# Strided attention heads with block-diagonal keys and values, in a fused sparse-attention and bilinear-FFN kernel

## The chip, the cores and the metric

The kernel runs on one core of a Trainium2 chip. The metric is the device time of one execution in microseconds; before the change the median of three runs is 328.93 (328.39 to 329.02). A core has TensorE (PE, matmuls, with its weight loads listed as PEld), VectorE (DVE), ScalarE (ACT), GpSimd (POOL), SyncE (SP) and 16 DMA engines. POOL and SP issue the transfers here.

## What is computed

Sparse attention over 8 batches, 8 heads, 576 positions and 64 values a head, and then a bilinear feed-forward layer. Heads 0 to 3 are local (a query sees the 32 latest positions), heads 4 to 7 strided (a query sees the earlier positions with the same remainder by 32).

```python
    mask_local = (rel >= 0) & (rel < stride)
    mask_strided = (rel >= 0) & (pos[None, :] % stride == pos[:, None] % stride)
    masks = np.stack([mask_local if h < H // 2 else mask_strided for h in range(H)], axis=0)
    scores = np.where(masks[None, :, :, :], scores, -1000000000.0)
...
    a = x @ w_a
    b = x @ w_b
    return (a * b @ w_out).astype(np.float32)
```

`x` is the attention's output, 4608 tokens of 512 values; `w_a` and `w_b` are 512 x 1536, `w_out` 1536 x 512.

## The kernel before, in words

**The order of the work.** Everything is one list of 144 slots, nine token tiles of 512 tokens with 16 slots each: 12 slots of `ffn_ab` (L584; per slot eight matmuls of 512 columns, L581, an ACT copy L598 and a DVE product L601 or L603) and four of the output product (`ffn_y` L762 for the first two tiles, `ffn_ys` L750 for the rest, a Strassen-like scheme whose sums DVE forms in `fast_s` L608, matmuls L686). Attention of batch b is woven into the slots of earlier tiles by hand: `STEPS` (L541) for batches 1 and 2, `LATER` (L546) for 3 to 7 give a position for each step; batch b's `LATER` positions count from slot 16(b-1), x.5 lies in the middle of slot x+1. `at` (filled from L884 on) gives, for each slot, the loads, transpositions and small jobs emitted behind it. Each engine runs its instructions in the order in which they are emitted. From slot 14 on, POOL first copies one element of the slot's result (`pace`, L936) before it issues what `at` has for the slot, so that loads don't run ahead.

**A batch from 2 on.** A batch has 8 units: unit u is pair c = u // 2 of heads, half u % 2; pairs 0 and 1 are local, 2 and 3 strided. A step "S" forms scores (`S_p`, L385) into the one score bank `st`, takes Exp (L393) into one of five buffers `p` and masks by a bitwise AND (L403). A step "V" (`step_VT`, L475) multiplies by the values (L486) into the one output bank `o`; half of the 128 weight columns are ones, so that partitions 64 to 127 of `o` hold the sums. ACT turns these into 1/sum by Ln and Exp (L495, L496), and DVE multiplies into `xT` (L500 for local, L502 for strided units), the FFN's input.

**Strided units before.** The 576 positions of a head are cut as 72 rows of 8 (`NP`, `RS`): in group r lie the positions that leave r by 8, 72 keys and 72 queries, and the mask `mask_s` keeps those with the same remainder by 32. A unit has 4 groups of 2 heads: eight score matmuls (weights: 128 columns of the transposed keys `kT`, moving: 72 queries of `qz`, zero outside of one head) and eight value matmuls (weights `vs`, 72 x 128; moving: 72 columns of `p`). Keys and queries are loaded by POOL (`load_qk`, L203, tiles `natk`, `natq`, once for all four heads, one DMA each head), transposed by DVE in 32 x 32 blocks, three instructions for each (`step_D`, L332), and sent by SP's DMAs (L342, L346) into `kT` and `qz`. Values are loaded by `load_vs` (L243), one DMA a head. Local heads go the same way: `kl`, `ql` (L212), transposed in two instructions (L327).

Batches 0 and 1 use other code for transposition and values, and are not changed; they share the buffers. `rezero` (L349), `zero_qz` (L113) and `fill_v` (L108) put zeros and ones into the buffers at their start or before the first use by a batch from 2 on. `mask_group` (L138) builds `mask_s` by a matmul.

Of the kernel before, what the change touches and what calls it, by code (L numbers as in the profile page):

```python
# [7 lines left out]
F32 = mybir.dt.float32  # L8
# [17 lines left out]
WCH = (0, 2, 5, 9, 12)  # L26
FAST_Y = (2, 3, 4, 5, 6, 7, 8)
# [3 lines left out]
def kernel(  # L31
# [44 lines left out]
    def qk_buf(nm):  # L76
        return (const.tile([128, 2, S], BF16, name=f"{nm}l"), const.tile([128, 2, RS * GP], BF16, name=f"{nm}s"))

    qz_buf = [[qk_buf(f"qz{i}{j}") for j in range(2)] for i in range(2)]
# [4 lines left out]
    nat_s = {nm: const.tile([128, 3, RS * D], BF16, name=f"nat{nm}") for nm in "qk"}  # L84
    p_buf = [const.tile([128, 2, PW], BF16, name=f"p{i}") for i in range(5)]
    vs_buf = [const.tile([NP, HL, RS, VW], BF16, name=f"vs{i}") for i in range(2)]
# [11 lines left out]
    def consts(i):  # L98
        if i == 0:
            for p in p_buf:  # L100
                nc.vector.memset(p[:, :, W:], 0.0)
        nc.vector.memset(kT_buf[i][0][:, :, 0:PAD], 0.0)
        nc.vector.memset(kT_buf[i][1], 0.0)
        nc.vector.memset(vl_buf[i][:, :, D:D + 1], 1.0)
        nc.vector.memset(vs_buf[i][:, :, :, D:D + 1], 1.0)
        nc.vector.memset(vl_buf[i][:PAD, 0, 0:D], 0.0)

    def fill_v(t):  # L108
        nc.gpsimd.memset(t[:, :, :, D:] if len(t.shape) == 4 else t[:, :, D:], 1.0)
# [28 lines left out]
    def mask_group(part):  # L138

        if part == 0:  # L140
            nc.scalar.copy(by4(nm_l[lo, :NP]), ident[lo, :NP // 4].unsqueeze(2).to_broadcast([32, NP // 4, 4]))
            nc.scalar.copy(by4(nm_l[up, :NP]), ident[up, 32:36].unsqueeze(1).to_broadcast([32, NP // 4, 4]))
            nc.scalar.copy(nm_l[64:], nm_l[:64])
        elif part == 1:
            nc.vector.tensor_scalar(nm_r[up], nm_l[up, :NP], 1.0, 8e9, op0=ALU.subtract, op1=ALU.mult)
            nc.vector.tensor_copy(nm_r[64:], nm_r[:64])
        else:
            mp = cur["misc"][:NP, 256:256 + NP]
            nc.tensor.matmul(mp, lhsT=nm_l[:, :NP], rhs=nm_r, start=True, stop=True)
            nc.vector.tensor_scalar(mask_s, mp, 0.0, -1.0, op0=ALU.is_equal, op1=ALU.mult)  # L150

# [35 lines left out]
    def load_qk(b, strided, heads=range(HL), names="kq"):  # L187
        for nm in names:
            src = {"k": k, "q": q}[nm]
            if b < FIRST_D:  # L190
                n, R, h0 = (NP, RS, HL) if strided else (96, RL, 0)
                w0 = {"k6": 0, "q6": 1536, "k8": 3072, "q8": 5120}[f"{nm}{R}"]
                if b not in shared:
                    shared[b] = nat.tile([128, FG * 5 * SW], BF16, tag="shared", name="shared")
                t = nats[b, nm, strided] = shared[b][:n, w0:w0 + HL * R * D].rearrange("p (h r d) -> p h r d", r=R, d=D)
                hs = slice(heads[0], heads[-1] + 1)
                nc.gpsimd.dma_start(out=t[:, hs], in_=src[b, h0:h0 + HL].rearrange("h (p r) d -> p h r d", r=R)[:, hs])  # L197
            elif strided:

                t = nat_s[nm]  # L200
                n = 32 if b == FIRST_D else YS
                for h in heads:
                    nc.gpsimd.dma_start(  # L203
                        out=t[32 * h:32 * h + n],
                        in_=bass.AP(tensor=src.tensor, offset=(b * H + HL + h) * S * D,
                                    ap=[[RS * D, n], [YS * RS * D, 3], [1, RS * D]]))
            else:
                if 0 in heads:
                    nats[b, nm, strided] = nat.tile([128, NY, D], BF16, tag=f"{nm}l", name=f"{nm}l")
                t = nats[b, nm, strided]  # L210
                for h in heads:
                    nc.gpsimd.dma_start(out=t[32 * h:32 * h + 32],  # L212
                                        in_=src[b, h].rearrange("(i y) d -> y i d", y=32))
            nats[b, nm, strided] = t
# [18 lines left out]
    def load_vs(b, heads=range(HL)):  # L233
        if b < FIRST_D:

            for z in range(2):
                t = blocks("k", z)
                nc.gpsimd.dma_start(out=t[:NP, :, :RS * D],
                                    in_=v[b, HL + 2 * z:HL + 2 * z + 2].rearrange("h (p r) d -> p h (r d)", r=RS))
                nats[b, "v", z] = t  # L240
            return
        for h in heads:
            nc.gpsimd.dma_start(out=vs_buf[b % 2][:, h, :, 0:D],  # L243
                                in_=v[b, HL + h].rearrange("(p r) d -> p r d", r=RS))
# [74 lines left out]

    def step_D(b, z, nm, part):  # L320
        src = nats[b, nm, z == 1]
        if part == 0:
            tl[b, z, nm] = blocks(nm, z)
        t = tl[b, z, nm]
        if z == 0:
            i = slice(NY // 2 * part, NY // 2 * (part + 1))
            nc.vector.transpose(t.rearrange("p h (i y) -> p i h y", i=NY)[:, i],  # L327
                                src[:, i].rearrange("p i (h d) -> p i h d", h=2))
            last = part == 1
        else:  # L330

            nc.vector.transpose(  # L332
                t.rearrange("p h (r c) -> p r h c", r=RS)[:, :, :, YS * part:YS * part + 32],
                src[:, part].rearrange("p (r h d) -> p r h d", r=RS, h=2))
            last = part == 2
        if last:
            for nm, c in {"k": (("k", 0),), "q": (("q", 0), ("k", 1), ("q", 1))}[nm]:
                t = tl[b, z, nm]
                for e in range(2):
                    if nm == "k":  # L340
                        dst = kT_buf[b % 2][z][64 * e:64 * e + 64, c]
                        nc.sync.dma_start(out=dst[:, PAD:] if z == 0 else dst[:, :RS * GP], in_=t[64 * c:64 * c + 64, e])  # L342
                        continue
                    for j in range(2):
                        r0 = 64 * c + 32 * j
                        nc.sync.dma_start(out=qz_buf[b % 2][j][z][64 * e + 32 * j:64 * e + 32 * j + 32, c],  # L346
                                          in_=t[r0:r0 + 32, e])

    def rezero(b):  # L349

        for j in range(2):
            for t in qz_buf[b % 2][j]:
                nc.gpsimd.memset(t[32:64] if j == 0 else t[64:96], 0.0)
# [35 lines left out]
    def S_x(b, u):  # L389
        c, half, M, n, G = unit(u)  # L390
        st = held.pop((b, "st", u))
        p = ps[b, u] = p_buf[(B * b + u) % 5]
# [15 lines left out]

    def step_S(b, u):
        S_px(b, u)  # L410
        S_m(b, u)
# [55 lines left out]
    def step_V(b, u):  # L467
        if b >= FIRST_D:
            step_VT(b, u)
# [5 lines left out]
    def step_VT(b, u):  # L475
# [4 lines left out]
        for i in range(G):  # L480
            for j in range(2):
                if c < 2:
                    vt = vl_buf[b % 2][:, (2 * c + j) * 6 + 3 * half + i]
                else:
                    vt = vs_buf[b % 2][:, 2 * (c - 2) + j, 4 * half + i]
# [4 lines left out]
        if c < 2:  # L490
            sums = o[64:, :, :W]
        else:

            sums, r = (t.rearrange(e, p=NP) for t, e in ((o[64:, :, :W], "d j (g p) -> d j p g"), (r, "d j (p g) -> d j p g")))
        nc.scalar.activation(r, sums, ACT.Ln)  # L495
        nc.scalar.activation(r, r, ACT.Exp, scale=-1.0)  # L496
        for j in range(2):
            dst = xT[64 * j:64 * j + 64, c, S * (b % XR):S * (b % XR + 1)]
            if c < 2:
                nc.vector.tensor_mul(dst[:, W * half:W * (half + 1)], o[:64, j, :W], r[:, j])  # L500
            else:
                nc.vector.tensor_mul(dst.rearrange("d (p r) -> d p r", r=RS)[:, :, G * half:G * (half + 1)],  # L502
                                     o[:64, j, :W].rearrange("d (g p) -> d p g", p=NP), r[:, j])
# [21 lines left out]
    def step_X(b, c):  # L525
# [18 lines left out]
             2: {20: "S0", 20.5: "S1", 21.5: "V0", 22: "S2", 23: "V1", 23.5: "S3", 24.5: "V2", 25: "S4", 26: "V3", 26.5: "S5",  # L544
                 27.5: "V4", 28: "S6", 28.5: "V5", 29: "S7", 29.5: "V6", 30.5: "V7"}}
    LATER = {-1: "S0", 0: "S1", 1: "V0", 2: "S2", 3: "V1", 4: "S3", 5: "V2", 6: "S4", 7: "V3", 8: "S5", 9: "V4", 10: "S6",  # L546
             11: "V5", 12: "S7", 12.5: "V6", 14: "V7"}
# [249 lines left out]
    with tc.manual_schedule(engines={ENG.PE, ENG.SP, ENG.Pool, ENG.DVE, ENG.Activation}):  # L797
# [87 lines left out]
        do(0, fill_v, vs_buf[0])  # L885
# [3 lines left out]
        for b in range(FIRST_D, B):  # L889
# [7 lines left out]
            else:  # L897
                for h in range(HL):
                    do(g0 + h + (2 if b == FIRST_D + 1 else -2), load_qk, b, False, (h,))
# [3 lines left out]
            gs = {2: (14, 14, 15, 15, 16, 16, 17, 17, 18, 18), 3: (8, 9, 10, 11, 12, 13, 14, 15, 16, 17)}.get(b) or (  # L903
                3, 5, 7, 9, 12, 13, 14, 15, 16, 17)
            for (z, nm, part), g in zip(((0, "k", 0), (0, "k", 1), (0, "q", 0), (0, "q", 1), (1, "k", 0), (1, "k", 1),
                                         (1, "k", 2), (1, "q", 0), (1, "q", 1), (1, "q", 2)), gs):
# [10 lines left out]
        do(28, fill_v, vs_buf[1])  # L917
# [52 lines left out]
```

## Time and profile before

| what | value |
|---|---|
| median of three runs | 328.93 us |
| span of the profiled execution | 326.3 us |
| PE busy, instructions | 320.6 us (98%), 2820 |
| DVE busy | 265.7 us (81%) |
| ACT busy | 202.7 us (62%) |
| POOL busy | 177.2 us (54%) |
| PE busy between 20 and 262 us | 242.00 of 242 us |
| POOL waiting at `pace` for DVE's `pf` (L601) | 80.7 us, 53 times |

The span runs from the first to the last instruction; the time of an execution also holds its start and end. The profile gives busy time by engine, the span in 40 slices, the chain of waits that ended last, and groups of instructions by line with their mean duration. A PE duration is that of one matmul from start to result; matmuls overlap, so the spacing of their starts tells what each costs. A line that is used by several shapes or tiles has a group for each in the list by form.

### The profile page before, as it was taken

The page shows a single profiled execution, that of the slowest core. Times are in us where ns is not written, and L with a number is a line of the kernel's source. Part 1 is how long each engine was busy: PE and PEld are TensorE (multiplying, and loading weights), DVE is VectorE, ACT ScalarE, POOL GpSimd, SP SyncE. Part 2 cuts the span into 40 slices and gives each one's busy share as a digit, 9 for nine tenths or more (in the row PEclk, how much of TensorE's full clock was granted, in tenths as well). Part 3 has the DMA queues.
Part 4 walks back from the last instruction along what each step waited for, and adds up shares of the span by engine and source line. Part 5 has one row for each costly group of instructions (what it writes and reads, how often), then busy time and mean ns, then how long its engine had stood idle before and what let it go on. Part 6 is the DMA issues. An engine that isn't in the chain of part 4 may idle for free.

```text
span 326.3 us, 7676 instructions
## 1 busy us (share of the span) xinstructions
PE 320.6 (98%) x2820; PEld 205.5 (63%) x2820; DVE 265.7 (81%) x509; ACT 202.7 (62%) x329; POOL 177.2 (54%) x295
## 2 busy tenths in 40 slices
PE   8999999999999999999999999999999999999995
PEld 6754655455555587557999985569555954584474
DVE  6766888889778999999999999999877845647562
ACT  6764775478778765777677757875677643313321
POOL 8935839599966655875577557853312031232021
PEclk9999999999999999999999999999999999999999
DMA  9999999999999798799979999898033022004004
GB/s 151 154 204 201 204 184 182 173 171 136 132 213 116 95 97 79 77 217 125 83 72 199 138 86 77 160 180 84 20 77 115 2 67 64 0 2 129 1 2 129
DMA packets 98869, 37.50 MB, mean 115 GB/s; under 512 B 76688, under 2 KB 96016, under 8 KB 98832
## 3 DMA queue, kind: packets, MB, share of 16 engines
q0 software_dynamic: 85968, 19.48, 64.5%
q1 hardware_dynamic: 12576, 17.34, 18.4%
q8 instruction: 22, 0.36, 0.4%
q10 hardware_dynamic: 288, 0.20, 0.2%
q14 instruction: 15, 0.12, 0.1%
HBM read 39.51 MB, written 9.44 MB: 150 GB/s over the span
## 4 chain that ended last, share of the span: by engine, by line
PE 96%; DMA 2%; POOL 0%; DVE 0%; issue 0%; POOLq 0%; ACT 0%; DVEq 0%
PE mm L581 56%; PE mm L686 17%; PE mm L768 6%; PE st L385 5%; PE o L486 4%; DMA shared<-in_q_dram 2%; PE mm L714 2%; PE o L442 1%; PE ab L581 1%; PE misc L154 1%; PE tp L511 1%; PE tp L296 1%; PE end L714 1%; PE tp L287 0%; POOL shared L197 0%
## 5 line engine op out<-in xcount | busy, mean ns | idle before, releaser
L581 PE MATMUL mm<-xT,wa_sb 128*128 128x512 bf16 (+1 forms) x472 | 110.3, 357 | 0.0
L581 PE MATMUL mm<-xT,wb_sb 128*128 128x512 bf16 (+1 forms) x472 | 110.3, 357 | 0.0
L598 ACT COPY a_sb<-mm 128x512 f32<-128x512 f32 x106 | 62.1, 586 | 48.3 <-PE mm L581 47.6
L936 POOL CAST pace<-pf 1x1 f32<-1x1 bf16 x84 | 31.4, 374 | 84.0 <-DVE pf L601 80.7
L581 PEld LDWEIGHTS <-wb_sb 128*128 128x128 bf16 x480 | 46.3, 98 | 44.0 <-issue 0.2
L601 DVE TENSOR_TENSOR pf<-a_sb,mm 128x512 bf16<-128x512 f32 x84 | 56.4, 672 | 17.0 <-PE mm L581 13.8
L581 PEld LDWEIGHTS <-wa_sb 128*128 128x128 bf16 x480 | 42.7, 98 | 31.3
L393 ACT ACTIVATE p<-st 128x576 bf16<-128x576 f32 (+1 forms) x64 | 41.6, 650 | 11.7 <-PE st L385 11.1
L495 ACT ACTIVATE xr<-o 64x576 f32<-64x576 f32 x48 | 31.1, 649 | 25.0 <-PE o L486 24.2
L686 PEld LDWEIGHTS <-ps 128*128 128x128 bf16 x360 | 34.6, 98 | 3.9
L496 ACT ACTIVATE xr<-xr 64x576 f32<-64x576 f32 x48 | 32.9, 685 | 1.5
L500 DVE TENSOR_TENSOR xT<-o,xr 64x288 bf16<-64x288 f32 x48 | 21.5, 447 | 7.2 <-ACT xr L496 6.7
L502 DVE TENSOR_TENSOR xT<-o,xr 64x288 bf16<-64x288 f32 x48 | 21.5, 448 | 6.2 <-ACT xr L496 5.1
L686 PE MATMUL mm<-wf,ps 128*128 128x256 bf16 x216 | 26.4, 273 | 0.0
L768 PE MATMUL mm<-wo_sb,pf 128*128 128x512 bf16 x96 | 23.4, 379 | 0.0
L403 DVE TENSOR_TENSOR p<-p,mask_l 128x576 int16<-128x576 int16 x32 | 22.2, 694 | 1.2 <-ACT p L393 1.1
L243 POOL DMA_DIRECT2D vs<-in_v_dram x24 | 19.7, 821 | 3.0 <-PE st L385 2.2
L212 POOL DMA_DIRECT2D kl<-in_k_dram x24 | 16.1, 671 | 5.5 <-issue 3.6
L212 POOL DMA_DIRECT2D ql<-in_q_dram x24 | 16.0, 666 | 5.2 <-DMA wo_sb<-in_moe_w_out_dram 3.8
L603 DVE TENSOR_TENSOR pf<-a_sb,mm 128x512 bf16<-128x512 f32 x22 | 14.9, 676 | 4.3 <-ACT a_sb L598 2.8
L936 POOL COPY pace<-y_sb 1x1 f32<-1x1 f32 x16 | 2.8, 177 | 27.8 <-ACT y_sb L669 15.1
L686 PE MATMUL mm<-wf,pf 128*128 128x256 bf16 x144 | 17.6, 273 | 0.0
(162 smaller groups left out, 502.1 us busy)
## 6 DMA issues: line engine op xcount, KB each, us to landing
out_dram<-y_sb SPq DMA_DIRECT2D x12, 512.0 KB, 4.6
out_dram<-y_sb SPq DMA_DIRECT2D x10, 256.0 KB, 3.3
vl<-in_v_dram POOLq DMA_DIRECT2D x6, 384.0 KB, 6.8
kl<-in_k_dram POOLq DMA_DIRECT2D x24, 72.0 KB, 3.0
ql<-in_q_dram POOLq DMA_DIRECT2D x24, 72.0 KB, 3.0
vs<-in_v_dram POOLq DMA_DIRECT2D x24, 72.0 KB, 3.7
wo_sb<-in_moe_w_out_dram POOLq DMA_DIRECT2D x4, 384.0 KB, 9.2
natk<-in_k_dram POOLq DMA_DIRECT2D x20, 72.0 KB, 3.3
```

The source lines that it names most:

```text
L212: nc.gpsimd.dma_start(out=t[32 * h:32 * h + 32], in_=src[b, h].rearrange("(i y) d -> y i d", y=32))
L393: nc.scalar.activation(p[:M, :, :W], st[:M, :, :W], ACT.Exp, scale=scale)
L403: nc.vector.tensor_tensor(pi, pi, mk, op=ALU.bitwise_and)
L495: nc.scalar.activation(r, sums, ACT.Ln)
L496: nc.scalar.activation(r, r, ACT.Exp, scale=-1.0)
L500: nc.vector.tensor_mul(dst[:, W * half:W * (half + 1)], o[:64, j, :W], r[:, j])
L581: nc.tensor.matmul(ps_[:, c0:c0 + n], lhsT=w[:, kk, 128 * f:128 * (f + 1)], rhs=xT[:, kk, x0:x0 + n], start=(kk == first and c0 == 0), sto ...
L598: nc.scalar.copy(a_sb, ab[0])
L601: nc.vector.tensor_mul(pf[:, f, :].rearrange("p (i a s) -> p a i s", i=2, s=16), halves(a_sb), halves(ab[1]))
L686: nc.tensor.matmul(bank[b][:, q], lhsT=lhs(g, q), rhs=rhs(g), start=new and q == 0 and g == 0, stop=g == FG - 1, skip_group_check=True)
L768: nc.tensor.matmul(ybank[j], lhsT=pf[:, f, 128 * j:128 * (j + 1)], rhs=wo_sb[:, f], start=(f == 0), stop=(f == FD - 1))
L936: nc.gpsimd.tensor_copy(pace, done)
```

## The change

For batches 2 to 7 the strided heads are cut otherwise. Positions are placed at 33 i + x (i = 0 to 17 the row of 32, x = 0 to 31 the remainder, x = 32 a zero pad), read as 54 keys n times 11 groups g: in a group lie the 54 positions with x in {g, g + 11, g + 22}. For a pair of heads one matmul takes 2 x 54 = 108 keys, both heads' keys block-diagonal in the weights (`kz`), against 54 queries of both heads: 11 score matmuls a pair (`pair_S`), their output 108 x 594. Both operands are read with a step of 11 elements. Exp is taken in two instructions (324 and 270 columns), the mask is one of 108 x 54 (`mask_z`). `pair_V` multiplies by block-diagonal values (`vz`, 108 x 128, head 0 in columns 0 to 63, head 1 in 64 to 127), 6 or 5 matmuls of 54 columns, and a constant block of ones (`ones_z`) gives the sums in one matmul of 324 or 270 columns. Ln and Exp then run on 128 partitions of 324 or 270, and two multiplications write both heads.

Steps S5 and S7 go (S4 and S6 do a pair each), V4 moves from position 9 to 8.5, S6 from 10 to 9, V5 from 11 to 10 (batch 2: V4 stays at 27.5, S6 at 28, V5 at 28.5). Strided keys and queries are loaded as the local ones are (576 pieces of a row a head, where it was 72, or 96 in batch 2), and transposed in two instructions instead of three, after a small memset of the pad; queries now go to `kT`, keys to `kz`. The value load of a head becomes three DMAs. The local loads of batch 3 move one slot earlier. New at the start: `zero_vz` in place of `fill_v` of `vs`, and `mask_pair` in three parts (slots 0, 15, 18: POOL memsets and selects; four ACT copies and a DVE operation; one matmul on PE and a DVE operation). In `rezero` one POOL memset clears the buffer of strided keys of both heads.

```diff
-                t = nat_s[nm]
-                n = 32 if b == FIRST_D else YS
-                for h in heads:
-                    nc.gpsimd.dma_start(
-                        out=t[32 * h:32 * h + n],
-                        in_=bass.AP(tensor=src.tensor, offset=(b * H + HL + h) * S * D,
-                                    ap=[[RS * D, n], [YS * RS * D, 3], [1, RS * D]]))
...
                 for h in heads:
                     nc.gpsimd.dma_start(out=t[32 * h:32 * h + 32],
-                                        in_=src[b, h].rearrange("(i y) d -> y i d", y=32))
+                                        in_=src[b, h + HL * strided].rearrange("(i y) d -> y i d", y=32))
...
         for h in heads:
-            nc.gpsimd.dma_start(out=vs_buf[b % 2][:, h, :, 0:D],
-                                in_=v[b, HL + h].rearrange("(p r) d -> p r d", r=RS))
+            p0, d0 = KH * (h % 2), D * (h % 2)
+            for e in range(3):
+                n = min(NG, 32 - NG * e)
+                nc.gpsimd.dma_start(
+                    out=vz_buf[b % 2][p0 + e:p0 + KH:3, h // 2, :n, d0:d0 + D],
+                    in_=bass.AP(tensor=v.tensor, offset=((b * H + HL + h) * S + NG * e) * D,
+                                ap=[[32 * D, NY], [D, n], [1, D]]))
...
+    def pair_S(b, u):
+        c = u // 2 - 2
+        kz = kz_of(b)[:, c].rearrange("p j (n g) -> p g (j n)", g=NG)
+        qT = kT_buf[b % 2][1][:, c, :NG * KH].rearrange("p (n g) -> p g n", g=NG)
+        st = pst.tile([128, 2, 512], F32, tag="st", name="st")
+        for g in range(NG):
+            nc.tensor.matmul(st[:KR, g // GB[0], KH * (g % GB[0]):KH * (g % GB[0] + 1)], lhsT=kz[:, g], rhs=qT[:, g],
+                             start=True, stop=True)
+        p = p_of(b, u).rearrange("p t w -> p (t w)")[:KR, :NG * KH]
+        ps[b, u] = ps[b, u + 1] = p
+        w = KH * GB[0]
+        for half in range(2):
+            f, n = w * half, KH * GB[half]
+            nc.scalar.activation(p[:, f:f + n], st[:KR, half, :n], ACT.Exp, scale=scale)
+        pi = p.bitcast(I16).rearrange("p (g n) -> p g n", n=KH)
+        nc.vector.tensor_tensor(pi, pi, mask_z.unsqueeze(1).to_broadcast([KR, NG, KH]), op=ALU.bitwise_and)
+
+    def pair_V(b, u):
+        c, half = u // 2, u % 2
+        g0, n = GB[0] * half, GB[half]
+        p = ps.pop((b, u))
+        o = psum4["o"].tile([128, 2, 512], F32, tag="o", name="o")
+        nc.tensor.matmul(o[:, 1, :KH * n], lhsT=ones_z[:KR], rhs=p[:, KH * g0:KH * (g0 + n)], start=True, stop=True)
+        for g in range(n):
+            nc.tensor.matmul(o[:, 0, KH * g:KH * (g + 1)], lhsT=vz_buf[b % 2][:KR, c - 2, g0 + g],
+                             rhs=p[:, KH * (g0 + g):KH * (g0 + g + 1)], start=True, stop=True)
...
+        nc.scalar.activation(r, by_x(o[:, 1, :KH * n]), ACT.Ln)
+        nc.scalar.activation(r, r, ACT.Exp, scale=-1.0)
...
-    LATER = {-1: "S0", 0: "S1", 1: "V0", 2: "S2", 3: "V1", 4: "S3", 5: "V2", 6: "S4", 7: "V3", 8: "S5", 9: "V4", 10: "S6",
-             11: "V5", 12: "S7", 12.5: "V6", 14: "V7"}
+    LATER = {-1: "S0", 0: "S1", 1: "V0", 2: "S2", 3: "V1", 4: "S3", 5: "V2", 6: "S4", 7: "V3", 8.5: "V4", 9: "S6",
+             10: "V5", 12.5: "V6", 14: "V7"}
...
-                    do(g0 + h + (2 if b == FIRST_D + 1 else -2), load_qk, b, False, (h,))
+                    do(g0 + h + (1 if b == FIRST_D + 1 else -2), load_qk, b, False, (h,))
...
-            gs = {2: (14, 14, 15, 15, 16, 16, 17, 17, 18, 18), 3: (8, 9, 10, 11, 12, 13, 14, 15, 16, 17)}.get(b) or (
-                3, 5, 7, 9, 12, 13, 14, 15, 16, 17)
+            gs = {2: (14, 14, 15, 15, 16, 17, 17, 18), 3: (8, 9, 10, 11, 12, 14, 15, 17)}.get(b) or (
+                3, 5, 7, 9, 12, 14, 15, 17)
```

## The prediction

> **What bounds the kernel now.** I read the page first, then the chain of waits, then the timeline of TensorE one instruction at a time.
>
> ```profile
> span 326.3 us, 7676 instructions
> ...
> PE   8999999999999999999999999999999999999995
> ...
> PEclk9999999999999999999999999999999999999999
> ...
> PE 96%; DMA 2%; POOL 0%; DVE 0%; issue 0%; POOLq 0%; ACT 0%; DVEq 0%
> ```
>
> TensorE (PE) is busy in every slice at full clock, and the chain that ended last is PE for 96%. A busy share can still hide waits, so I took the start of every matmul from the trace and subtracted, from start to next start, what its columns explain: the 512-column ones follow each other at 216 ns, the 256-column ones at 109 ns, that is columns / 2.4 + 2.5 ns. From 20 us to the end the remainders sum to about 0.5 us. So from there on PE never waits for anybody. **Time is the sum of PE's steps**; time saved on ACT, DVE or POOL is worth nothing, time added there costs only once it makes PE wait. The batches that change (2 to 7) run from 65 to 262 us.
>
> **What the strided heads cost PE today.** In the timeline of PE (start, duration, engine, line, tiles, form):
>
> ```profile
> 140.00 0.20 PE L385 MATMUL st<-qz00s,kT0s 128*128 128x72 bf16 x1
> 140.03 0.20 PE L385 MATMUL st<-qz01s,kT0s 128*128 128x72 bf16 x1
> ...
> 140.26 0.38 PE L581 MATMUL mm<-xT,wa_sb 128*128 128x512 bf16 x1
> ```
> ```profile
> 145.96 0.42 PE L486 MATMUL o<-p,vs 72*128 72x72 bf16 x8
> 146.22 1.03 PE L581 MATMUL mm<-xT,wa_sb 128*128 128x512 bf16 x4
> ```
>
> The duration of one (0.20 us) is latency; what counts is start to start. Eight score matmuls of 72 columns take 140.00 to 140.26 = 0.26 us, 32.4 ns each; eight value matmuls 145.96 to 146.22, the same. A batch has four score and four value units: 8 x 0.26 = **2.08 us**.
>
> **What they cost PE after, values.** A pair has 11 value matmuls of 54 columns, and two of 324 and 270 columns for the sums. 54 columns would stream in 25 ns, but each also needs a weight load. The smallest matmuls of the trace show that floor (L444 has one column, L442 64):
>
> ```profile
> 15.66 0.16 PE L444 MATMUL sum<-vl,p 72*128 72x1 bf16 x1
> 15.69 0.19 PE L442 MATMUL o<-tk,p 72*128 72x64 bf16 x1
> 15.72 0.17 PE L444 MATMUL sum<-vl,p 72*128 72x1 bf16 x1
> ```
>
> A matmul of one column is followed after some 26.5 ns (unrounded starts). So 22 x 26.5 = 0.58 us a batch; sums 324/2.4 + 2.5 = 138 and 270/2.4 + 2.5 = 115 ns, times two pairs, 0.51 us. Values: **1.09 us**, against 1.04 before. The sums eat what the fewer matmuls give.
>
> **After, scores.** 22 matmuls of 54 columns instead of 32 of 72; the columns alone would give 22 x 25. But their weights have 108 columns, not 128, and both operands are read 11 elements (22 bytes) apart. The groups of weight loads (last number before the second bar is the mean ns of one):
>
> ```profile
> L486 PEld LDWEIGHTS <-vs 72*128 72x128 bf16 x192 | 9.3, 98 | 3.2 <-DVE xT L502 0.3
> ...
> L290 PEld LDWEIGHTS <-shared 96*64 96x64 bf16 x24 | 0.6, 109 | 0.8 <-DMA shared<-in_k_dram 0.6 <-DMA shared<-in_q_dram 0.2
> ...
> L149 PEld LDWEIGHTS <-nml 128*72 128x72 bf16 x1 | 0.1, 113 | 0.0
> ```
>
> Narrower loads take longer: 128 columns 98 ns (96 where they follow each other fastest), 64 columns 109, 72 columns 113. From 64 to 72 that is 0.4 to 0.5 ns a column, so an estimate for 108 is 113 + 36 x 0.42 = 128 ns, 31 ns over the 97 of a 128-column load. A load starts when the matmul before starts (2 ns after, in the listing) and the next matmul waits for it, so the pitch becomes 26.5 + 31 = **57 ns**. Ends: 26.5 if a 108-column load behaves like one of 128; 47 if the floor of 26.5 is not the load's own time but an issue floor, and only 108 x 0.42 = 45 + 2 counts; and, if the 22-byte step slows the read, more. For the step the nearest rows are copies of 576 elements out of PSUM, read 192 bytes apart (kT0l) and contiguously (kT0s) on DVE, and both ways on ACT:
>
> ```profile
> L307 DVE COPY kT0l<-tp x2: 758/758/758, 5.3 to 7.7; 128x576 bf16<-128x576 bf16 x2
> L307 DVE COPY kT0s<-tp x2: 444/450/457, 10.8 to 13.2; 128x576 bf16<-128x576 bf16 x2
> ...
> L523 ACT COPY xT<-tp x8: 627/640/647, 14.5 to 57.3; 128x576 bf16<-128x576 bf16 x8
> ```
>
> A factor of 1.68 on DVE, 1.0 on ACT. On PE the trace has only weights read 4 bytes apart (L686, 98 ns, no loss). So the factor lies between 1.0 and 1.68, and the pitch between 57 and 57 x 1.68 = 96 ns. I take 57: the row on PE itself is the nearest.
>
> Scores per batch: 22 x 0.057 = 1.25 us (ends 0.58, 1.03, 2.11). With values: 2.34 against 2.08, **+0.26 us a batch, +1.6 us in six** (ends -2.5, +0.2, +6.7). Break-even is at (2.08 - 1.09) / 22 = 45 ns.
>
> The rules of the skill. The Trainium skill, "TensorE: Matmul & The Clock Gate", section on weight-path perf modes, says that the fast weight load is on only when the weights have exactly 128 columns; the rows above show it for 64 and 72, none for 108. Its section on LDWEIGHTS puts a load at columns / 1.2 ns, 90 ns for 108, which by that page would make the scores 22 x 92 = 2.0 us and the change an estimated +6 us. The trace's step from 64 to 72 columns is half as steep, and I go by the trace. "SBUF — State Buffer", its note on cachelines (section on the DMA port swizzle), says that reads which touch a new 16-byte line each time pay a penalty because two hits per line are needed; taken as a factor of two that would be about 100 ns and +7 us. No row here shows it for PE.
>
> **Waits that the change adds.** (a) V4 moves from position 9 to 8.5, and S5 no longer lies between V3 and V4. One output bank (o) serves both: V4 may start when V3's second multiplication has ended.
>
> ```profile
> 141.99 0.42 PE L486 MATMUL o<-p,vl 128*128 128x96 bf16 x6
> ...
> 144.01 0.91 DVE L500 TENSOR_TENSOR xT<-o,xr 64x288 bf16<-64x288 f32 x2
> ```
>
> V3's chain (matmuls, Ln 0.65, Exp 0.69, two multiplications) ends 2.77 us after its start in most batches, 2.92 here (144.91). After the change PE reaches V4 after 0.26 + 1.73 + 0.86 = 2.85 us. So nothing to 0.2 us, five times; behind a waiting V4 stands all of PE. I take 0.3 us in all, bounds 0 and 0.9. V5 and later follow shorter chains (324-column Ln and Exp instead of 576), so they gain slack. (b) The new mask's matmul on PE: 0.1 us. (c) POOL issues 12 v loads a batch for 4. A v load costs it 0.82 us, one with as many packets from 32 rows 0.66, one of 72 packets 0.61; a third of a load I put at 0.62, so 4 x (1.86 - 0.82) = 4.2 us more. POOL's idle behind them:
>
> ```profile
> 158.19 0.18 POOL L936 COPY pace<-y_sb 1x1 f32<-1x1 f32 x1 [2.65 <-ACT y_sb L671]
> ...
> 164.94 0.27 POOL L936 CAST pace<-pf 1x1 f32<-1x1 bf16 x1 [1.66 <-DVE pf L601]
> ```
>
> 2.65 + 0.54 us before slot 14 leaves it 1 us late, and 1.66 at slot 16 absorbs that; the last local k load keeps its 1.6 us of slack before its transposition. Batch 3 is tight (POOL has no idle from 65 to 81 us, and DVE once waited 0.57 us for kl at 76.15): its natk lands some 2.7 us later, at 85.0, and is transposed at 84.85. DVE's wait is then a few tenths, and V5 to V6 have 0.9 us to hide it: nothing. (d) q and k of the strided heads come in 576 packets of 128 bytes instead of 72 of 1 KB; both land 3.0 to 3.4 us after issue, and in the crowded stretch at 50 us one kl load lands every 0.5 us, no slower than natk: nothing.
>
> **Gains that are worth nothing.** ACT falls from 4 x (0.65 + 0.65 + 0.69) = 7.9 to about 4.9 us a batch, DVE from 4 x 0.44 + 8 x 0.45 + 6 x 0.70 = 9.6 to about 6.8. PE waits for neither now.
>
> **Sum.** 1.6 + 0.3 + 0.1 = +2.0 us on a span of 326.3. The profiled execution's span is 2.6 us below the median of 328.93, which is start and end around it and doesn't change. Forecast **330.9 us**.
>
> **Rivals.** (1) The 108-column loads are as fast as 128-column ones and the step costs nothing: pitch 26.5, -2.5 + 0.1 + 0.3 = -2.1, **326.9**. For it: columns and matmuls really fall by a quarter. Against: the 109 and 113 ns rows. It decides from a pitch under 42 ns, with (a) and (b) paid. (2) The 22-byte step slows the read as on DVE: pitch 96, +6.7 + 0.4, **336.0**. For: 758 against 450; against: ACT's 640 and L686's 98. (3) POOL becomes late: if a third of a v load costs the full 0.82, batch 3's natk lands 6.6 us later, DVE blocks some 4 us and PE about 3: **334**; more if the thirds wait for each other to land (3.7 us each). Against: POOL idles 80 us at its pace copies.
>
> **How the numbers follow.** Forecast 0.42, rival 1 0.22, rival 2 0.28, rival 3 0.08. Range 326.5 (rival 1 without stalls) to 336.8 (rival 2 with 0.9 of stalls at V4). The forecast's own range is 329.3 (47 ns) to 331.6. A measurement here can tell about 0.2% (0.66 us) from no change; the low end of the forecast's range, 0.12, falls within it. So faster 0.22, same 0.12, slower 0.66.
>
> **What would show it.** In the profile after: the starts of pair_S's matmuls, 57 ns apart (26 or 96 for the rivals); their weight loads near 128 ns; value matmuls 26 ns apart; PE still busy throughout; V4's wait for xT under 0.2 us; no DVE wait for natk over 1 us. The forecast fails if the score pitch lies elsewhere: each 10 ns is 1.3 us.

## The result, and the profile after

The changed kernel takes 346.78 us (median of four runs, 346.30 to 350.19) against 328.98 for the kernel before beside it: a ratio of 1.056, 95% interval 1.051 to 1.061. That is 18 us slower, and above the predicted range. The profiled execution has a span of 344.6 us, 18.3 more than before. The lines of its page that answer to those of before (the span, PE's busy share in 40 slices, the granted clock, the chain of waits by engine and by line):

```profile
span 344.6 us, 7510 instructions
...
PE   8999999999999999999999999999999999999995
...
PEclk9999999999999999999999999999999999999999
...
PE 93%; POOL 2%; DMA 2%; issue 1%; DVE 0%; ACT 0%; POOLq 0%; DVEq 0%
PE mm L651 52%; PE mm L756 16%; PE st L452 7%; PE mm L838 6%; PE st L418 2%; PE o L565 2%; DMA vl<-in_v_dram 2%; PE mm L784 2%; POOL shared L231 1%; PE o L524 1%; PE o L471 1%; PE o L469 1%; PE ab L651 1%; PE end L784 1%; PE tp L581 1%
```

The kernel is bound as before: PE busy in every slice, at full clock, the chain on PE. PE runs 95 matmuls fewer (2820 records before, 2725 in the packed variants below, which have the same number; 32 are missing in this trace) and is busy 16.5 us longer (337.1 for 320.6). So it is PE's own work that grew. The new item in the chain is `st` L452, the score matmuls of `pair_S`, with 7% of the span, 24 us. The timeline of PE in batch 4 (start, duration, engine, line, tiles, form, count):

```profile
153.13 0.81 PE L651 MATMUL mm<-xT,wb_sb 128*128 128x512 bf16 x3
153.78 2.12 PE L452 MATMUL st<-kT0s,zs 128*108 128x54 bf16 x11
155.72 0.40 PE L651 MATMUL mm<-xT,wa_sb 128*128 128x512 bf16 x1
```
```profile
157.46 0.28 PE L469 MATMUL o<-p,vs 108*128 108x270 bf16 x1
157.58 0.29 PE L471 MATMUL o<-p,vs 108*128 108x54 bf16 x5
157.72 1.02 PE L651 MATMUL mm<-xT,wa_sb 128*128 128x512 bf16 x4
```

The eleven score matmuls take 153.78 to 155.72 = 1.94 us, start to next start; the forecast was 11 x 57 ns = 0.63. In the trace one follows the other after **187 ns** (the pitch, start to next start; only the second of a group comes sooner, after 80). The value matmuls, with the same 54 columns, behave as forecast: the sums' 270 columns 0.12 us, then five in 0.14 us. What differs most between the two is the weight load. The groups of weight loads, by form (last number before the second bar: mean ns of one):

```profile
L452 PEld LDWEIGHTS <-zs 128*108 128x108 bf16 x132 | 25.9, 278 | 1.2
...
L471 PEld LDWEIGHTS <-vs 108*128 108x128 bf16 x132 | 6.6, 97 | 2.6 <-issue 1.0
```

278 ns where 128 was forecast. Twelve groups of 1.93 us are 23.2 us, the values 6 x 1.11 = 6.7; before, both were 6 x 2.08 = 12.5. That makes +17.4 of the 18.3 us. The rest is mostly the wait at V4, in the timelines of PE and PEld (in brackets the idle time ahead and its releaser):

```profile
152.47 0.30 PE L469 MATMUL o<-p,vs 108*128 108x324 bf16 x1
152.76 0.32 PE L471 MATMUL o<-p,vs 108*128 108x54 bf16 x6
```
```profile
152.44 0.10 PEld L469 LDWEIGHTS <-vs 108*128 108x128 bf16 x1 [0.30 <-DVE xT L573]
```

At the other places of this trace 141 ns pass from a matmul of 324 columns to the next; here it is 290. V4 waits 0.12 to 0.15 us for V3's multiplication (L573) in each of batches 3 to 7: 0.71 us.

The first question for the chip: is it the narrower weights (108 columns for 128), the step of 11 elements in the weights, or the one in the queries? My theory now was the step; the rivals were the width alone, and the block-diagonal shape as such.

### The profile page after: what moved, and what is told of

Read it like the earlier page. It is cut to its first block, busy times and chain, and to the rows that moved or that the text cites. A ratio compares the mean times of both kernels' runs of the same rounds, so it can differ in the third digit from the quotient of the medians.

```text
span 344.6 us, 7510 instructions
## 1 busy us (share of the span) xinstructions
PE 337.1 (98%) x2693; PEld 223.0 (65%) x2725; DVE 249.4 (72%) x498; ACT 184.9 (54%) x333; POOL 196.7 (57%) x346
## 4 chain that ended last, share of the span: by engine, by line
PE 93%; POOL 2%; DMA 2%; issue 1%; DVE 0%; ACT 0%; POOLq 0%; DVEq 0%
PE mm L651 52%; PE mm L756 16%; PE st L452 7%; PE mm L838 6%; PE st L418 2%; PE o L565 2%; DMA vl<-in_v_dram 2%; PE mm L784 2%; POOL shared L231 1%; PE o L524 1%; PE o L471 1%; PE o L469 1%; PE ab L651 1%; PE end L784 1%; PE tp L581 1%
## 5 line engine op out<-in xcount | busy, mean ns | idle before, releaser
L1009 POOL CAST pace<-pf 1x1 f32<-1x1 bf16 x83 | 22.0, 265 | 101.1 <-DVE pf L671 100.8
L671 DVE TENSOR_TENSOR pf<-a_sb,mm 128x512 bf16<-128x512 f32 x84 | 56.6, 674 | 19.0 <-PE mm L651 15.5
L274 POOL DMA_DIRECT2D vs<-in_v_dram x72 | 47.1, 659 | 2.3 <-PE mm L651 2.3
L573 DVE TENSOR_TENSOR xT<-o,xr 64x288 bf16<-64x288 f32 x48 | 21.6, 450 | 13.8 <-ACT xr L570 13.5
L426 ACT ACTIVATE p<-st 128x576 bf16<-128x576 f32 (+1 forms) x40 | 26.0, 651 | 9.9 <-PE st L418 9.6
L452 PEld LDWEIGHTS <-zs 128*108 128x108 bf16 x132 | 25.9, 278 | 1.2
L569 ACT ACTIVATE xr<-o 64x576 f32<-64x576 f32 x24 | 15.5, 647 | 12.8 <-PE o L565 11.6
L476 ACT ACTIVATE xr<-o 128x324 f32<-128x324 f32 (+1 forms) x24 | 10.0, 418 | 21.3 <-PE o L471 21.3
L484 DVE TENSOR_TENSOR xT<-o,xr 128x216 bf16<-128x216 f32 (+1 forms) x24 | 9.3, 389 | 14.8 <-ACT xr L477 14.8
L756 PE MATMUL mm<-wo_sb,ps 128*128 128x256 bf16 x144 | 17.5, 272 | 0.0
```

Source lines behind the costliest of these rows:

```text
L274: nc.gpsimd.dma_start(out=vz_buf[b % 2][p0 + e:p0 + KH:3, h // 2, :n, d0:d0 + D], in_=bass.AP(tensor=v.tensor, offset=((b * H + HL + h) * ...
L426: nc.scalar.activation(p[:M, :, :W], st[:M, :, :W], ACT.Exp, scale=scale)
L452: nc.tensor.matmul(st[:KR, g // GB[0], KH * (g % GB[0]):KH * (g % GB[0] + 1)], lhsT=kz[:, g], rhs=qT[:, g], start=True, stop=True)
L671: nc.vector.tensor_mul(pf[:, f, :].rearrange("p (i a s) -> p a i s", i=2, s=16), halves(a_sb), halves(ab[1]))
L756: nc.tensor.matmul(bank[b][:, q], lhsT=lhs(g, q), rhs=rhs(g), start=new and q == 0 and g == 0, stop=g == FG - 1, skip_group_check=True)
L1009: nc.gpsimd.tensor_copy(pace, done)
```

## Experiments: which operand, which property

The first four kernels change only where `pair_S` reads. Number and shape of the instructions stay, but for 128 weight columns in the fourth; with a packed operand the scores are those of other positions.

**Both operands packed, 108 columns.**

```diff
-        kz = kz_of(b)[:, c].rearrange("p j (n g) -> p g (j n)", g=NG)
-        qT = kT_buf[b % 2][1][:, c, :NG * KH].rearrange("p (n g) -> p g n", g=NG)
+        kz = kz_of(b)[:, c].rearrange("p j n -> p (j n)").rearrange("p (g m) -> p g m", g=NG)
+        qT = kT_buf[b % 2][1][:, c, :NG * KH].rearrange("p (g n) -> p g n", g=NG)
```

> The score matmuls of pair_S read both operands packed: 108 neighbouring weight columns and 54 neighbouring queries in place of a step of 11 elements (so the scores are those of other positions). Counts, widths and waits stay. Theory step (the 22-byte step is what costs): start to start falls from 187 ns to between 47 and 57 ns, 132 matmuls save 17 to 18 us, time 329 to 330. Theory width (a load of 108 columns is not overlapped with the streaming): stays near 187 ns, 346.8.

Measured: 329.45 us, ratio 1.0017 (1.0005 to 1.0029), span 327.7. The pitch is 50 ns. The weight loads by form, and the group in the timeline of PE:

```profile
L452 PEld LDWEIGHTS <-zs 128*108 128x108 bf16 x132 | 8.4, 130 | 2.1
```
```profile
83.34 0.69 PE L452 MATMUL st<-kT0s,zs 128*108 128x54 bf16 x11
83.87 0.38 PE L838 MATMUL mm<-wo_sb,pf 128*128 128x512 bf16 x1
```

278 ns become 130, eleven matmuls 0.53 us, and 17 of the 18 us are gone. The steps are the cause. The rest of the change is nearly neutral (0.7 us over the kernel before, 0.2 to 1.0): ACT (184.8 us busy) and DVE (248.0) are relieved by 18 us each against before, and the time does not fall.

**One operand packed.** The second kernel has only the first line of that edit (weights packed), the third only the second (queries packed).

> Only the weights of pair_S are packed, the queries keep the step of 11 (scores of other positions). In the trace of the changed kernel a weight load starts 113 ns after the matmul before it, and the next matmul 74 ns after the load. Theory step, with the two costs adding: the 113 ns are the queries' and stay, the 74 become about 30, pitch 115 to 145, time 337 to 341. If the weights alone were the cause: pitch 57, 329.6. Theory width: 187 ns, 346.8.

> Only the queries of pair_S are packed, the weights keep the step of 11 (scores of other positions). Theory step, with the two costs adding: the 113 ns fall to some 25, the 74 stay, pitch 75 to 100, time 332 to 335. If the queries alone were the cause: pitch 57, 329.6. Theory width: 187 ns, 346.8.

Measured: weights packed 336.56 us, 1.023 (1.022 to 1.025), pitch 100 ns; queries packed 345.48 us, 1.050 (1.049 to 1.052), pitch 185 ns. The groups in the timelines of PE, weights packed and then queries packed:

```profile
142.89 1.26 PE L452 MATMUL st<-kT0s,zs 128*108 128x54 bf16 x11
143.97 1.04 PE L651 MATMUL mm<-xT,wa_sb 128*128 128x512 bf16 x4
```
```profile
145.53 2.03 PE L452 MATMUL st<-kT0s,zs 128*108 128x54 bf16 x11
147.41 1.02 PE L651 MATMUL mm<-xT,wa_sb 128*128 128x512 bf16 x4
```

1.08 and 1.88 us for eleven. I had expected the costs of the two operands to add; they do not. Alone the queries' step gives 100 and the weights' 185, both together 187: the larger one counts, which fits with loads running beside matmuls; their exact interplay was not tried further. Packing the queries alone saves almost nothing.

**Both packed, 128 columns.** Both operands are packed, and twenty columns of a neighbouring group are loaded as well, whose results are not used. The matmul of the edit:

```diff
-            nc.tensor.matmul(st[:KR, g // GB[0], KH * (g % GB[0]):KH * (g % GB[0] + 1)], lhsT=kz[:, g], rhs=qT[:, g],
-                             start=True, stop=True)
+            nc.tensor.matmul(st[:, g // GB[0], KH * (g % GB[0]):KH * (g % GB[0] + 1)], lhsT=kz[:, 105 * g:105 * g + 128],
+                             rhs=qT[:, g], start=True, stop=True)
```

> Both operands of pair_S packed as in the first, and 128 weight columns instead of 108 (20 of them of the next group, their rows unread; scores of other positions). If a load of 108 columns is slower than one of 128: pitch 26.5 ns against 47 to 57, and the time 2.7 to 4 us under that of the kernel with 108 packed columns, 325 to 326.5, below the kernel before. If the width does not matter once the columns are packed: both at 26.5 ns and the same time.

Measured: 327.16 us, 0.9945 (0.9928 to 0.9963), span 324.9, pitch 27.5 ns. Loads by form, and the timeline:

```profile
L452 PEld LDWEIGHTS <-zs 128*128 128x128 bf16 x132 | 5.3, 97 | 2.4
```
```profile
138.75 1.03 PE L651 MATMUL mm<-xT,wb_sb 128*128 128x512 bf16 x4
139.62 0.46 PE L452 MATMUL st<-kT0s,zs 128*128 128x54 bf16 x11
139.91 1.02 PE L651 MATMUL mm<-xT,wa_sb 128*128 128x512 bf16 x4
```

More columns load faster: 20 added columns take the pitch from 50 to 27.5 ns. Width is the smaller part of the loss: twelve groups of 0.30 us for 0.53 are 2.7 us, and by the medians it is 2.3. With both mended the scheme gains what fewer matmuls can give: 2 x 0.30 + 1.11 - 2.08 = -0.37 us a batch, -2.2 in six, +0.8 at V4 in this trace, so -1.4. The span falls by 1.4, the time by 1.8 (1.2 to 2.4).

## Experiments: how the cost depends on the step

Is a step dear as such, or from a certain width on? These kernels read one operand packed and the other with a step that differs from batch to batch, one run each (their times have no interval; the pitches are read from the two groups of each batch and agree within 1.5 ns). The queries' scan; the weights' does the same to `lhsT`, and the last two take 128 weight columns:

```diff
+        step = (2, 4, 7, 8, 9, 10)[b - FIRST_D]
...
-            nc.tensor.matmul(st[:KR, g // GB[0], KH * (g % GB[0]):KH * (g % GB[0] + 1)], lhsT=kz[:, g], rhs=qT[:, g],
+            nc.tensor.matmul(st[:KR, g // GB[0], KH * (g % GB[0]):KH * (g % GB[0] + 1)], lhsT=kz[:, g], rhs=qT[:, g:g + step * (KH - 1) + 1:step],
```

> Weights of pair_S packed (108 columns), queries read with another step in each batch: 2, 4, 7, 8, 9 and 10 elements in batches 2 to 7 (scores of other positions); the pitch of each batch's score matmuls is read from the trace. Known: 50 ns at step 1, 100 at step 11. Theory threshold (what costs is that every element lies in another line of some size): 50 ns up to some step, then a jump to 100 that stays. Theory proportion (cost grows with the bytes spanned): about 50, 60, 75, 80, 87, 93.

> Queries of pair_S packed, weights (108 columns) read with another step in each batch: 2, 4, 7, 8, 9 and 10 elements in batches 2 to 7 (scores of other positions). Known: 50 ns at step 1, 185 at step 11. Theory threshold: 50 ns up to some step, the same as for the queries, then a jump to 185 that stays. Theory proportion: about 63, 90, 130, 145, 158, 170.

> As the scan of the queries, but with 128 packed weight columns, so that the load (27 ns) hides less: steps 3, 4, 5, 6, 8 and 12 in batches 2 to 7 (scores of other positions). At 108 columns, steps 2 and 4 showed 50 and 52 ns and step 7 87. If the cost sets in when fewer than two elements lie in 16 bytes (a step over 4): 27 ns at 3, up to 35 at 4, and a rise between 5 and 8 to 100. If it grows with the step: 30, 36, 45, 55, 73, 110.

> Queries packed, 128 weight columns with steps 2, 3, 4, 6, 8 and 9 in batches 2 to 7 (scores of other positions). With 108 columns step 2 cost 51 ns and step 4 already 100. If a load of 128 columns (four at a time) meets the same limit: 27 ns at step 2 and a rise from 3 or 4 on, to some 60 at step 8, a quarter of the slope of 108 columns; if wide loads lose their speed altogether with a step: as with 108, 100 at step 4 and 200 at step 8.

Pitch in ns by the step in elements of two bytes:

| step | 1 | 2 | 3 | 4 | 5 | 6 | 7 | 8 | 9 | 10 | 11 | 12 |
|---|---|---|---|---|---|---|---|---|---|---|---|---|
| queries, weights 108 packed | 50 | 50 | | 52 | | | 87 | 98 | 100 | 100 | 100 | |
| weights 108, queries packed | 50 | 52 | | 100 | | | 173 | 198 | 193 | 187 | 185 | |
| queries, weights 128 packed | 27.5 | | 39 | 52 | 64 | 75 | | 98 | | | | 98 |
| weights 128, queries packed | 27.5 | 27.5 | 27 | 33 | | 47 | | 60.5 | 60 | | | |

Times: 334.09, 341.54, 332.57 and 328.49 us. The eleven matmuls at step 8 in the timelines of PE, one line from each kernel, in the order of the rows (the second number is start to last result, 0.15 to 0.18 us longer than start to next start):

```profile
176.10 1.24 PE L453 MATMUL st<-kT1s,zs 128*108 128x54 bf16 x11
```
```profile
178.30 2.25 PE L453 MATMUL st<-kT1s,zs 128*108 128x54 bf16 x11
```
```profile
210.18 1.24 PE L453 MATMUL st<-kT0s,zs 128*128 128x54 bf16 x11
```
```profile
207.91 0.80 PE L453 MATMUL st<-kT0s,zs 128*128 128x54 bf16 x11
```

Three things are to be seen. First, above what stays hidden the cost rises in proportion to the step, and it is flat from 8 elements, 16 bytes, on (for weights it even falls, from 198 to 185 ns, which stays unexplained). This fits a cost for each piece of 16 bytes that is touched, the same for both operands: 98 / 54 = 1.81 ns for queries at step 8, 198 / 108 = 1.83 for weights; 54 pieces cost about 100 ns whether they are 54 queries at step 8 or 108 weights at step 4. That the piece has 16 bytes is read from the bend of these curves alone. Second, a load of 128 columns does the same nearly four times as fast: 60.5 / 128 = 0.47 ns. Third, what stays hidden depends on the other work: 108 weights at step 2 cost no more than the packed load's own 50 ns, 128 weights none up to step 3 (27 ns), but queries at step 3 already cost 39.

So no step from 8 on is much cheaper than 11. The table also offers a half measure that no run tried: 128 columns with both steps kept. An estimate is 100 ns instead of 187, the larger of 60 for the weights (step 9) and 100 for the queries (step 11).

## Experiments: can the packing be had?

The packed layout with 128 columns would be the faster kernel if the right positions came to lie packed.

**DVE writes the new order.** The transposition itself places a position at 18 x + i, remainder by remainder; a group is three neighbouring remainders, and its 54 positions lie side by side. Mask, value loads and output views follow. One kernel with 108 columns, one with 128. Here the weights hold the right positions and are block-diagonal. Core of the edit:

```diff
-        nc.vector.transpose(tile_of(nm).rearrange("p h (i y) -> p i h y", i=NY)[:, i, :, :32],
+        nc.vector.transpose(tile_of(nm).rearrange("p h (y i) -> p i h y" if z else "p h (i y) -> p i h y", i=NY)[:, i, :, :32],
```

> The change with another order of positions: the transposition by DVE writes by remainder (position 18 x + i), so that a group is three neighbouring remainders and both operands of its score matmul are packed; each score matmul still has 108 weight columns; pair_V needs one multiplication instead of two. All else as in the changed kernel. Theory step: score pitch 50 ns as in the run with packed slices, time 329 to 330. If the packing only moves the cost (DVE transposing with a step in its output, SP's keys in pieces of 108 bytes): DVE or the landing of kz becomes late and the time is over 331.

> As the previous, with 128 weight columns read (20 of the next group, their output rows unread). Theory step plus width: score pitch 27 ns, 132 matmuls save 3.0 us against 108 columns, 326 to 327.5, under the kernel before. If width matters only by chance of the layout: 329 to 330 as with 108.

Measured: 348.34 us, 1.059 (1.0535 to 1.0645), and 350.24, 1.063 (1.058 to 1.068). The score pitch is 50 and 27 ns as meant: the block-diagonal shape as such costs nothing, the third rival above. But DVE pays. Groups of the 128-column kernel by form, strided against local, PE's waits (total us, times, longest), and the granted clock in 40 slices:

```profile
L366 DVE STREAM_TRANSPOSE tq<-natq 128x576 bf16<-128x576 bf16 x12 | 31.8, 2652 | 0.2
...
L366 DVE STREAM_TRANSPOSE tk<-kl 128x576 bf16<-128x576 bf16 x12 | 9.3, 774 | 0.2
```
```profile
PE mm L648 <- DVE pf L668: 7.0, 9, 0.9
PE st L421 <- DVE vs L184: 5.4, 1, 5.4
PE st L455 <- DMA zs<-tk: 2.5, 4, 0.8
```
```profile
PEclk9999999969999999999999999999999999999999
```

Written 36 bytes apart, a transposition lasts 2.65 us, not 0.79. DVE has 81% of the span in the 108-column kernel and would have room for it, but in the order of the work its products `pf` stand behind each transposition, and PE waits for `pf` to free its bank: 0.6 to 1.0 us lost each of nine times, and 5.4 us once, in batch 2, for the mask's operation (L184), which stands behind two transpositions. After that long wait the granted clock was lower (0.68 between 75 and 80 us): from 72.8 to 78 us matmuls of 512 columns followed each other at 426 ns, not 216, another 2.5 us. The 128-column kernel also waits for keys that land late (`zs`, four times), so it gains nothing over the one with 108.

**ACT reorders.** The transposition stays; a copy on ACT reads with step 11 and writes each group packed, ahead of the DMAs (128 columns). The second kernel also puts V4 at position 9, ahead of S6, and V5 at 10.5, against the wait at V4. Core of the two edits:

```diff
+        if last and z:
+            t = nat_w[nm].rearrange("p (h m) -> p h m", h=2)
+            nc.scalar.copy(t.rearrange("p h (g n) -> p h g n", n=KH), tile_of(nm).rearrange("p h (n g) -> p h g n", g=NG))
+            tl[b, z, nm] = t
...
-    LATER = {-1: "S0", 0: "S1", 1: "V0", 2: "S2", 3: "V1", 4: "S3", 5: "V2", 6: "S4", 7: "V3", 8.5: "V4", 9: "S6",
-             10: "V5", 12.5: "V6", 14: "V7"}
+    LATER = {-1: "S0", 0: "S1", 1: "V0", 2: "S2", 3: "V1", 4: "S3", 5: "V2", 6: "S4", 7: "V3", 9: "V4 S6",
+             10.5: "V5", 12.5: "V6", 14: "V7"}
```

> The change with its own transpositions (786 ns each on DVE, output packed in blocks of 32), and one ACT copy each for keys and queries of a batch that puts the 11 groups one behind the other (1188 elements, read with a step of 11); keys then go to kz in pieces of 54, and the score matmuls read both operands packed, 128 weight columns (20 unread rows). Theory: score pitch 27 ns; two copies of about 1.2 us a batch fit into ACT's idle time; 326.5 to 328, under the kernel before, as with 128 packed columns of wrong positions (327.2). If ACT pays for the step as PE does (2 us or more a copy) or becomes late: PE waits for PSUM banks, over 329.

> As the previous, with V4 back at position 9 (ahead of S6) and V5 at 10.5. The wait of V4 for V3's multiplication (some 0.15 us of PE in each of batches 3 to 7 in the traces so far) should go: 0.5 to 0.8 us less than the previous. If that wait was already hidden: the same.

Measured: 354.20 us, 1.076 (1.070 to 1.083), and 352.33, 1.071 (1.0655 to 1.0768). The first of the two: the copy by form, PE's waits, and the place in the timelines of ACT and PE.

```profile
L371 ACT COPY natk<-tk 128x1188 bf16<-128x1188 bf16 x6 | 14.1, 2348 | 8.1 <-DVE tk L366 5.6 <-DMA vs<-in_v_dram 2.5
...
L133 ACT COPY zs<-qz00l 128x1280 bf16<-128x1280 bf16 x1 | 1.3, 1257 | 0.0
```
```profile
PE mm L658 <- ACT a_sb L675: 15.2, 7, 2.2
PE mm L658 <- ACT y_sb L746: 5.5, 3, 1.8
```
```profile
142.06 2.33 ACT L371 COPY natq<-tq 128x1188 bf16<-128x1188 bf16 x1 [1.80 <-DVE tq L366]
144.41 0.59 ACT L675 COPY a_sb<-mm 128x512 f32<-128x512 f32 x1
```
```profile
145.05 1.02 PE L658 MATMUL mm<-xT,wa_sb 128*128 128x512 bf16 x4 [2.22 <-ACT a_sb L675]
```

The strided copy lasts 2.35 us where one of 1280 contiguous elements lasts 1.26. ACT stood idle for 1.8 us ahead of it, for the transposition; then `a_sb` waits behind the copy, and PE behind `a_sb`. ACT is busy for 59% of the span, and PE still loses some 2 us at ten of the twelve copies. Moving V4 removes its wait (PE's weight load at L476 waited 1.4 us for `xT` in four places, and no longer does), but the two times' intervals overlap, so what that is worth in time stays open.

None of these beats the kernel before. What might: the packed order without an instruction of over 2 us in front of `pf` or `a_sb`, for instance the transposition or copy cut in pieces. That was not tried.

## Why the prediction was wrong

- **What bounds the kernel: right.** Time was the sum of PE's steps in the changed kernel too. From the measured pitches the sum gives each variant's span against 326.3: both packed 2 x 0.53 + 1.11 - 2.08 = +0.09 us a batch, +0.5, and +0.7 at V4, so +1.2 (measured 327.7, +1.4); weights packed +7.9 (measured +8.4); as changed +18.1 (measured +18.3).
- **The failed step: "What they cost PE after, scores", the factor of the 22-byte step.** I bounded it by 1.0 and 1.68, from copies out of PSUM on DVE and ACT and from weights read 4 bytes apart (L686), and took 1.0 because that row was on PE itself. Measured, it is 185 / 50 = 3.7 for the weights and 100 / 50 = 2.0 for the queries. The row on PE was right and told nothing: at a step of 2 elements the chip shows no loss at all (27.5 ns), at 11 it shows the whole. Neither of my ends was a bound; the rows were of other engines, another memory or a fifth of the step. With 187 ns in place of 57 its own sum gives 22 x 0.187 + 1.09 - 2.08 = +3.1 us a batch, +18.7 in six (17.4 measured, as the first pitch of each eleven is shorter). Rival 2 had the mechanism, but its 96 ns came from DVE's 1.68.
- **The width: right.** 47 to 57 ns was said for 108 columns without the step; 50 was measured on packed ones, and 27.5 on 128. The load was put at 128 ns and lasts 130.
- **Values: right.** 1.11 us a batch for 1.09: pitch 26.7 ns, the sums 141 and 119 ns where 138 and 115 were counted.
- **The wait at V4: right in place, low in size.** 0.71 us, within 0 to 0.9, against 0.3 taken. Both terms came out as counted: V3's chain ends 2.76 us after its start, V4's first matmul starts after 2.85 to 2.88. What waits is V4's weight load: it starts only 0.05 us after the chain's end, 0.03 to 0.06 ahead of its matmul, where V6's load is 0.11 ahead. The sum had compared the matmul alone.
- **POOL and the transfers: right.** A third of a v load costs POOL 0.66 us (0.62 taken), POOL's busy time rises by 19.5 us, and no wait for `natk` or `natq` shows on DVE. Rival 3 did not come.
- **Relief of ACT and DVE: worth nothing, right.** The kernel with both operands packed shows it alone.
- **Start and end: wrong, and small.** The 2.6 us are the median less the span of another, faster execution. In executions with both on record it is 2.1 to 2.2 us before and 1.7 after. That is why the time of the packed kernel rises by 0.7 us where its span rises by 1.4.
- **The sum's ends: a slip.** By its own terms the upper end of the range is 328.93 + 6.7 + 0.1 + 0.9 = 336.6, not 336.8, and that of the forecast 331.5, not 331.6. Neither matters against 346.78.

With 50 ns in place of 57 and no factor my own sum would be 22 x 0.050 + 1.09 - 2.08 = +0.11 us a batch, +1.1 with the waits taken: the forecast fits the kernel with packed operands (+0.7 us of time, +1.4 of span), and misses the changed one by the factor.

Two statements of the Trainium skill can now be weighed. "TensorE: Matmul & The Clock Gate", section on weight-path perf modes, says that the fast load is on for 128 weights, packed or strided: the runs agree on 128 (27.5 against 50 ns) and show that a step keeps a good part of it (60 against 198 ns at step 8) but is not free. "SBUF — State Buffer", note on cachelines in the section on the DMA port swizzle, says that lines have 16 bytes and that bf16 may be read up to 8 elements apart for free: the flat part from 8 elements on agrees with the line, the free part does not hold for PE here, where queries at step 3 already cost 39 ns for 27.5 and the cost rises with every further element up to 8.

## What to carry to other kernels

Count what a matmul reads, not only what it multiplies: here an operand with a step cost PE in proportion to the 16-byte pieces it touched, most for the 108 weight columns, and fewer matmuls cost more than many. A weight load of 108 columns became faster as one of 128, though 20 of them were not needed. And a bound for an access pattern must come from the same engine and at least the same step; where no such row exists, the range has to say so by its width.

## What was not expected of the hardware

- One rate fits both operands where the step shows: 1.8 ns per 16-byte piece, for 54 queries and for 108 weights alike, and 0.47 ns with 128 weight columns; the two operands' costs overlap instead of adding (187 ns together, 185 and 100 alone).
- A 32 x 32 block transposition on DVE whose output is written 36 bytes apart takes 2652 ns for 774 with 576 elements; an ACT copy reading 22 bytes apart 2348 ns for 1188 elements, against 1257 for 1280 contiguous ones.
